# Two segments' closing work on VectorE issued behind the next segment's last key tile

## The chip, the cores and the metric

The kernel runs on one core of a Trainium2 chip. The metric is the device time of one execution in microseconds (us). Five engines each work through a queue of their own in a fixed order: TensorE (PE) multiplies matrices into PSUM, VectorE (DVE) and ScalarE (ACT) read PSUM and work on SBUF, GpSimd (POOL) fills and loads a little, and SyncE (SP) issues most DMA transfers. They wait for each other through semaphores. An instruction that waits holds up everything behind it in its own queue.

## The reference

Two attention layers over 2048 tokens, 32 heads of width 18, are computed and laid side by side. Layer A has one key and value head for all query heads; layer B splits the tokens into four segments of 512 and carries a memory from one to the next:

```python
# A: p = softmax(q k^T * Dh**-0.5) over all 2048 keys; out_A = (p v) wo
for s in range(4):                        # B, one segment of 512 tokens
    p = softmax(qs ks^T * scale + mask)
    a_dot = p vs
    pq = phi(qs)                          # phi(t) = t + 1 if t > 0 else exp(t)
    a_mem = (pq M) / (pq z + 1e-6)
    outs.append(g * a_mem + (1 - g) * a_dot)
    pk = phi(ks)
    M = M + pk^T vs                       # the memory, per head 18 x 18
    z = z + pk.sum(over tokens)
# out = concat(out_A, concat(outs) wo_B)
```

## The kernel before, in words

The program has two stages. The first (to about 289 us) computes all projections, and the second runs the attention blocks, the divisions and the output products from a table that is written out by hand. The change touches the first stage alone. The two are divided by a branch (L627, L628), which every engine passes.

In the first stage the order on each engine is not written by hand. A scheduler takes the instructions as the program issues them, with their dependencies, and lays each engine's queue out ahead of time. What the program issues earlier tends to stand earlier; an instruction that is issued in another place can therefore move many others. `tc.issue_after(x)` makes what is issued inside it depend on `x`. `pin` keeps an instruction in program order.

The loop at L414 does one segment `s` of layer B per turn:

- **Five key tiles** `t` (L449). `proj` (L253) multiplies 14 pairs of rounded parts into a PSUM tile `pj` of 126 x 512. There are four buffers of `pj`, so a tile's first matmul waits until the tile four places earlier has been read. Of `pj`, VectorE takes the maximum of each row (`kmB`, L459) and a masked copy of it (`kbB`, L463); ScalarE rounds it and VectorE forms the remainder (`qp`, L122 and L123, stored to `kB` or `qB` by SP at L127). Then `phi` (L394 to L401) runs two steps on ScalarE (`ph_e`, L397 and L398) and one on VectorE (L400, result `kf`, for the last tile `qf`). These steps take turns on one `pj`, so each waits for the one before it.
- In the next turn of `t`, `natural` (L424) transposes `kf` on TensorE into the one PSUM buffer `tr` (L427), and VectorE copies that to `pkN` (L428). Behind the five tiles `natural` does the same for `qf`, and L519 transposes `kn` into the same buffer `tr`.
- **The next segment's input**, `xr`, has three buffers of 128 x 512. SP loads it (L196), and VectorE rounds it (`xh`, L209) and forms the remainder (`xl`, L215; L217 for the short last part). A buffer can be loaded again when the remainder is formed.
- **Values** (L493): eight tiles of 14 matmuls (L503), copied to `vch` by ScalarE (L505).
- **Four query tiles** (L539): `proj` again, with `aq` (L433), `qp`, and for `s` > 0 `phi`, result `qf`.
- **The close of the segment.** TensorE forms `pu` (PSUM buffer `nd`, L566) and the memory products `pm` (PSUM buffer `mm`, L592). Of `pu`, VectorE makes the shifts: `fm` (L567), `sht` (L132) and two steps on `shp` (L134, L135), and SP stores `shB` (L571). Of `pm` it gathers the memory: L601, for `s` > 0 a sum L608, seven copies to `Mst` (L613), `zc` (L614) and five `zst` (L616), and SP stores `mzB` (L618, L619).

In segments 1 and 2 the memory is only stored for later (`from_memory`, L435, in these segments stores `qf` to `qfB`). Segment 3 reads `Mst` and `zst` directly.

Of the kernel before, what the change touches and what calls it, by code (L numbers as in the profile page):

```python
# [8 lines left out]
F32 = mybir.dt.float32  # L9
# [5 lines left out]
ALU = mybir.AluOpType  # L15
AX = mybir.AxisListType
# [5 lines left out]
NSEG, L = 4, 512  # L22
C = 512
# [38 lines left out]
LATE_ASK, ASK = (1, 2), 20  # L62


def below(rows, r0):
    return slice(rows.start + r0, rows.stop + r0, rows.step)
# [9 lines left out]
def attention_pair_kernel(ctx, tc, a_xT, a_w, a_wo, b_xT, b_w, b_wo, b_beta, ident_d, hmask_d, bmask_d, cmask_d, sel_d, zmask_d, selx_d, sely_d, out):  # L76
    nc = tc.nc
# [8 lines left out]
    qA = [dram(f"qA{c}", [H, DH, 2, C], F32) for c in range(NCH)]  # L86
    kA = dram("kA", [DH, 2, S], F32)
# [4 lines left out]
    shA = [shAs[:, H * c : H * c + H] for c in range(NCH)]  # L92
# [12 lines left out]
    ones_d = dram("ones_d", [2, S], F32)  # L105
# [23 lines left out]
    def shift_parts(pool, u, neg_scale, n, R):  # L129

        t = pool.tile([128, C], F32, name="sht", bufs=1)
        nc.vector.tensor_scalar(t[:R, :n], u, neg_scale, None, op0=ALU.mult)  # L132
        sp = pool.tile([128, 2, C], F32R, name="shp", bufs=1)
        nc.vector.tensor_copy(sp[:R, 0, :n], t[:R, :n])  # L134
        nc.vector.tensor_tensor(sp[:R, 1, :n], t[:R, :n], sp[:R, 0, :n].bitcast(F32), op=ALU.subtract)  # L135
        return sp

    def load_q(st, q, h0):

        for hf, r0 in enumerate(HALF):  # L140
            hs = slice(h0 + hf, h0 + 8, 2)
            nc.sync.dma_start(st[r0 : r0 + 36].bitcast(F32), q[hs].rearrange("h d j t -> (d j) h t"))
            nc.sync.dma_start(st[r0 + 36 : r0 + 54].bitcast(F32), q[hs, :, 0, :].rearrange("h d t -> d h t"))

# [12 lines left out]
    with ExitStack() as ph:  # L157
# [236 lines left out]
        def phi(src, R, nm, bufs, hold=lambda ins: ins):  # L394

            e = p2.tile([128, C], F32, name="ph_e", bufs=2)
            hold(nc.scalar.activation(e[:R], src, AF.Relu, scale=-1.0))  # L397
            hold(nc.scalar.activation(e[:R], e[:R], AF.Exp, scale=-1.0))  # L398
            f = p2.tile([128, C], F32, name=nm, bufs=bufs)
            hold(nc.vector.scalar_tensor_tensor(f[:R], src, 0.0, e[:R], op0=ALU.max, op1=ALU.add))  # L400
            return f  # L401

        def loose_flag():

            fm1 = pt.tile([128, 1], F32, name="fm1", bufs=1)
            nc.vector.tensor_reduce(fm1, fm, axis=AX.X, op=ALU.max)
            pf = ps.tile([128, C], F32, name="nd", bufs=2)
            nc.tensor.transpose(pf[0:1, 0:128], fm1, ident)
            fm2 = pt.tile([1, 2], F32, name="fm2", bufs=1)
            nc.vector.tensor_reduce(fm2[:, 0:1], pf[0:1, 0:128], axis=AX.X, op=ALU.max)  # L410
            nc.vector.tensor_scalar(fm2[:, 1:2], fm2[:, 0:1], float(BOUND_OK), None, op0=ALU.is_gt)
            nc.vector.tensor_copy(flag, fm2[:, 1:2])

        for s in range(NSEG):  # L414
            xh, xl = nx[:2]
            last = s == NSEG - 1
# [18 lines left out]
            def from_memory(t):  # L435
                R = RT[t]
                if s in LATE_ASK:
                    nc.sync.dma_start(qfB[s][:R, t], fs[t][:R])
                    return
                pn = ps.tile([128, C], F32, name="mm", bufs=1)  # L440
                nc.tensor.matmul(
                    pn[:R], Mst[:R, t].rearrange("p h d -> p (h d)")[:, :R], fs[t][:R], start=True, stop=True
                )
                nm = p2.tile([128, C], F32, name="nm", bufs=2)
                nc.vector.tensor_scalar(nm[:R], pn[:R], gt[:R, t : t + 1], None, op0=ALU.mult)
                nc.sync.dma_start(numB[s][126 * t : 126 * t + R], nm[:R])
# [30 lines left out]
                        load_wpart(11 + t)  # L477
            if s:
                from_memory(4)
            if s == 0:  # L480
                nc.vector.memset(gt, 0.0)
                for t, lo, hi, n in [(t, H0[t], H0[t] + HT[t], DH) for t in range(5)] + [(5, 0, 28, 4), (6, 28, 32, 32)]:
                    pin(
                        nc.gpsimd.dma_start(
                            gt[: n * (hi - lo), t : t + 1], b_beta[lo:hi][:, None].to_broadcast([hi - lo, n])[:, :, None]
                        )
                    )
# [76 lines left out]
            for t in range(5):  # L564
                R = RT[t]
                nc.tensor.matmul(pu[32 * (t % 4) : 32 * (t % 4) + 32], kbB[:R, t], aqs[t][:R], start=t < 4, stop=t > 0)  # L566
            nc.vector.tensor_reduce(fm[:, 1 + s : 2 + s], pu, axis=AX.X, op=ALU.max)  # L567
            if last:
                loose_flag()
            sp = shift_parts(pt, pu, -BOUND_UP, C, 128)  # L570
            sent = nc.sync.dma_start(shB[s].rearrange("j r t -> r j t"), sp.bitcast(F32))  # L571
            if last:
                for i in range(4):
                    values(i, 1)

            with tc.issue_after(sent.ins):
                if s == 1:
                    for r0 in HALF:
                        for rows, j in KROWS:
                            nc.sync.dma_start(kstA[below(rows, r0)].bitcast(F32), kA[:, j])  # L580
                        nc.sync.dma_start(kstA[r0 + KP : r0 + KR].bitcast(F32), ones_d)
                if s == 2:
                    load_q(st0, qA[0], 0)
                    load_shift(st0, shA[0], slice(0, 8))
            if s < NSEG - 1:
                pm = ps.tile([128, C], F32, name="mm", bufs=1)[:, : 5 * 3 * VW].rearrange("p (t m) -> p t m", t=5)
                for t in range(5):
                    for i in range(4):
                        for g in range(4 if t < 4 else 3):
                            rows = slice(32 * g, min(32 * g + 32, RT[t]))  # L590
                            h = H0[t] + FIRST[t == 4][g]
                            nc.tensor.matmul(  # L592
                                pm[rows, t],
                                pkN[:, t, i, rows],
                                vch[:, i, h : h + 3, :].rearrange("p h d -> p (h d)"),
                                start=i == 0,
                                stop=i == 3,
                            )
                new = mx if s else Mbd
                for n, (R, ts) in enumerate(((126, slice(0, 4)), (72, slice(4, 5)))):  # L600
                    nc.vector.tensor_tensor(  # L601
                        new[:R, ts].rearrange("p t h d -> p t (h d)"),
                        pm[:R, ts],
                        bands[:R, n : n + 1].rearrange("p t h d -> p t (h d)").to_broadcast([R, ts.stop - ts.start, 3 * VW]),
                        op=ALU.mult,
                    )
                if s:
                    nc.vector.tensor_tensor(Mbd[:126], Mbd[:126], mx[:126], op=ALU.add)  # L608
                for ts in (slice(0, 4), slice(4, 5)):
                    for g in range(4 if ts.start < 4 else 3):  # L610
                        rows = slice(32 * g, min(32 * g + 32, RT[ts.start]))
                        w = FIRST[ts.start == 4][g]
                        nc.vector.tensor_copy(Mst[rows, ts, w : w + 3], Mbd[rows, ts, :, 1:VW])  # L613
                nc.vector.tensor_reduce(zc[:126], Mbd[:126, :, :, 0], axis=AX.X, op=ALU.add)  # L614
                for t in range(5):
                    nc.vector.tensor_scalar(zst[: RT[t], t], zmask[: RT[t], t], zc[: RT[t], t : t + 1], None, op0=ALU.mult)  # L616
                if s + 1 in LATE_ASK:
                    nc.sync.dma_start(mzB[:, s, :, :126], Mst.rearrange("p t h d -> p t (h d)"))  # L618
                    nc.sync.dma_start(mzB[:, s, :, 126:], zst)  # L619
            if s == 0:  # L620
                pin(nc.scalar.activation(gt, gt, AF.Exp, scale=-1.0))
                pin(nc.vector.tensor_scalar(gt, gt, 1.0, None, op0=ALU.add))
# [685 lines left out]
```

## Time and profile before

| what | number |
|---|---|
| median of 3 runs | 1407.49 us (1407.48 to 1408.29) |
| the profiled execution's own time | 1409.33 us |
| its span, first to last instruction | 1407.6 us |
| granted TensorE clock, mean | 0.996 |
| TensorE busy over the span | 99% |
| VectorE busy over the span | 74% |
| ScalarE busy over the span | 85% |
| first stage ends (branch, L628) | about 289 us |

A row of the timeline gives the start, the duration, the engine, the line, the operation and how often it is merged; in brackets stands how long the engine was idle just before, and what released it. Matmuls are pipelined: they start about 0.23 us apart though each is shown with 0.39 us. A row of the windows gives each engine's busy time in a stretch, then the granted clock (PEclk), the share of DMA engines that are busy and GB/s.

### The profile page before, as it was taken

The numbers are of one execution on the slowest core, as the hardware profiler recorded it, in microseconds if no ns is written. First come the engines' busy times: TensorE is split into PE (matmuls) and PEld (weight loads), VectorE is DVE, ScalarE is ACT, GpSimd is POOL, SyncE is SP. The second block draws the span as 40 slices with busy tenths as digits, with TensorE's granted clock in tenths as the row PEclk, the third lists the DMA queues.
The fourth block names the chain that finished last, engine by engine and source line by source line (L and its number), as shares of the span: only waits on it lengthen the run. The fifth ranks groups of instructions, "written<-read, shape, count | busy, mean of one in ns | idle before, by whom it ended". The sixth has DMA issues, their size and how long they took to land.

```text
span 1407.6 us, 41232 instructions
## 1 busy us (share of the span) xinstructions
PE 1387.5 (99%) x17468; PEld 839.3 (60%) x17468; DVE 1045.2 (74%) x1557; ACT 1198.5 (85%) x1479; POOL 233.5 (17%) x335
## 2 busy tenths in 40 slices
PE   9999999989999999999999999999999999999998
PEld 6787888745554555555555555555555555555558
DVE  6656456466787779687878878777879778887883
ACT  4543434479999999999999999999999999999991
POOL 2442000003302310412110122113010220001002
PEclk9999999989999999999999999999999999999999
DMA  9766546567465345332312452333103321120022
GB/s 273 259 214 189 168 145 221 182 176 229 138 202 181 118 130 182 103 115 85 112 58 71 133 158 60 94 105 92 51 30 96 110 75 43 31 68 18 18 67 105
DMA packets 90726, 172.70 MB, mean 123 GB/s; under 512 B 14576, under 2 KB 22889, under 8 KB 90110
## 3 DMA queue, kind: packets, MB, share of 16 engines
q1 hardware_dynamic: 84122, 160.01, 36.7%
q0 software_dynamic: 1664, 4.78, 1.3%
q10 hardware_dynamic: 4752, 5.24, 1.1%
q8 instruction: 138, 2.26, 0.7%
q14 instruction: 50, 0.41, 0.1%
HBM read 99.32 MB, written 70.67 MB: 121 GB/s over the span
## 4 chain that ended last, share of the span: by engine, by line
PE 66%; DVE 4%; DMA 3%; ACT 3%; issue 2%; SPq 1%; POOL 0%; DVEq 0%; ACTq 0%
PE O L996 31%; PE E L948 19%; PE F L799 11%; ACT P L966 3%; PE E L956 3%; DVE W L963 2%; PE E L1209 2%; DMA stA<-qA 1%; DMA stB<-shB 1%; DMA stB<-qB 1%; PE F L855 1%; DMA oB<-oe 1%; DVE sm L748 0%; DVE PD L928 0%; DMA stB<-kB 0%
## 5 line engine op out<-in xcount | busy, mean ns | idle before, releaser
L966 ACT ACTIVATE P<-E 128x1024 f32<-128x1024 f32 (+1 forms) x800 | 786.7, 1073 | 4.7 <-PE E L948 4.5
L963 DVE COPY W<-E 128x1024 f32<-128x1024 f32 (+2 forms) x416 | 453.3, 1090 | 144.5 <-PE E L948 84.7
L996 PE MATMUL O<-P,VA 128*32 128x256 f32 x7504 | 508.1, 380 | 0.0
L966 ACT ACTIVATE P<-W 128x1024 f32<-128x1024 f32 (+1 forms) x330 | 369.2, 1119 | 5.8 <-DVE W L963 5.4
L996 PEld LDWEIGHTS O<-P,VA 128*32 128x32 f32 x7504 | 259.2, 110 | 138.7 <-issue 6.1
L948 PE MATMUL E<-stA,kstA 56*128 56x512 f32 x1920 | 316.9, 430 | 2.0 <-ACT P L966 1.8
L948 PEld LDWEIGHTS E<-stA,kstA 56*128 56x128 f32 x1920 | 155.0, 184 | 158.6 <-issue 94.6
L971 POOL TENSOR_SCALAR_AFFINE_SELECT P<-P 128x256 f32<-128x256 f32 (+1 forms) x192 | 94.6, 493 | 415.0 <-ACT P L966 376.8
L783 POOL TENSOR_TENSOR o<-o,rb 126x512 f32<-126x512 f32 (+1 forms) x55 | 72.9, 1351 | 438.1 <-DVE PD L929 185.1
L799 PE MATMUL F<-woB,o 126*32 126x192 f32 (+1 forms) x1920 | 126.6, 338 | 0.0
L996 PE MATMUL O<-PD,VA 128*32 128x256 f32 x688 | 88.9, 379 | 0.0
L799 PEld LDWEIGHTS F<-woB,o 126*32 126x32 f32 (+1 forms) x1920 | 38.6, 108 | 74.9 <-issue 69.7
L996 PE MATMUL O<-P,vseg 128*32 128x256 f32 (+2 forms) x1536 | 81.4, 344 | 0.1
L922 DVE TENSOR_SCALAR PD<-E 128x512 uint32<-128x512 f32 x86 | 59.2, 689 | 24.7 <-PE E L948 16.1
L1005 DVE COPY oe<-O 128x512 f32<-128x512 f32 x64 | 44.3, 692 | 42.5 <-PE O L996 41.5
L253 PE MATMUL pj<-xh,wBh 128*126 128x512 f32 x180 | 72.1, 401 | 0.0
L253 PE MATMUL pj<-xh,wBl 128*126 128x512 f32 x180 | 71.5, 397 | 0.0
L122 ACT CAST qp<-pj 126x512 fp32r<-126x512 f32 (+1 forms) x54 | 31.0, 583 | 43.1 <-DVE kmB L459 26.8
L123 DVE TENSOR_TENSOR qp<-pj,qp 126x512 fp32r<-126x512 f32 (+1 forms) x54 | 36.8, 685 | 37.5 <-ACT qp L122 37.5
L799 PE MATMUL F<-woA,o 126*32 126x192 f32 (+1 forms) x960 | 63.9, 338 | 0.0
L996 PEld LDWEIGHTS O<-P,vseg 128*32 128x32 f32 x1536 | 48.8, 109 | 24.5 <-issue 1.9
L956 PE MATMUL E<-stB 56*128 56x256 f32 (+3 forms) x512 | 61.4, 348 | 2.0 <-ACT P L966 1.3
(198 smaller groups left out, 1575.1 us busy)
## 6 DMA issues: line engine op xcount, KB each, us to landing
stB<-kB SPq DMA_DIRECT2D x96, 144.0 KB
stB<-qB SPq DMA_DIRECT2D x32, 288.0 KB
stA<-qA SPq DMA_DIRECT2D x30, 288.0 KB
oA<-oe SPq DMA_DIRECT2D x32, 256.0 KB
oB<-oe SPq DMA_DIRECT2D x32, 256.0 KB
qA<-qp SPq DMA_DIRECT2D x16, 504.0 KB
kB<-qp SPq DMA_DIRECT2D x16, 504.0 KB
qB<-qp SPq DMA_DIRECT2D x16, 504.0 KB
```

The lines of the kernel that those rows point to most:

```text
L123: hold(nc.vector.tensor_tensor(qp[:R, 1, :n], src, qp[:R, 0, :n].bitcast(F32), op=ALU.subtract))
L253: nc.tensor.matmul(dst, w[:, c0 : c0 + M], x, start=i == 0, stop=i == len(ops) - 1)
L783: ins = tc.keep_in_program_order(nc.gpsimd.tensor_tensor(dst, a, b, op=op))
L799: nc.tensor.matmul(dst[32 * j : 32 * j + 32], parts[ab, c][: RT[t], t, r0 : r0 + 32], wo[ab][: RT[t], t, c0 : c0 + n], start=start, stop=stop,
L922: v.tensor_scalar(y, e, EXP_A, EXP_B, op0=ALU.mult, op1=ALU.add)
L948: nc.tensor.matmul(e[:, j], kstA[rows, 128 * kt : 128 * kt + 128], st[rows, h, :], start=True, stop=True)
L956: nc.tensor.matmul(e[:, j, c0 : c0 + 512 - 128 * k], st[rows, 4 + h, ks], st[rows, h, 128 * k :], start=True, stop=True)
L963: gate.append(nc.vector.tensor_copy(src[:, hs, :n], e[:, hs, :n]))
L966: nc.scalar.activation(p[:, hs, :n], src[:, hs, :n], AF.Exp, scale=SCALE)
L971: nc.gpsimd.affine_select(diag, diag, pattern=[[0, 2], [0, m], [1, 128]], base=0, channel_multiplier=-1, compare_op=ALU.is_ge, fill=0.0)
L996: nc.tensor.matmul(o[32 * j : 32 * j + 32, q0 : q0 + n], v, p[:, j % 2, p0 : p0 + n], start=m == hf == 0, stop=last and hf == 1,)
L1005: nc.vector.tensor_copy(osb, o)
```

## The change

The close of a segment is put into two functions, `shifts` (from L567 to the loads behind the store of `shB`) and `collect` (L599 to L619). In segments 0 and 1 they are kept in a list and issued in the next turn of the loop, behind its five key tiles, as dependent on the last tile's `phi` (`summed`). The last one in is taken first, so `collect` comes ahead of `shifts`. In segment 2 both are issued where they were; segment 3 has only the shifts, where they were. No instruction is added or removed; `pu` and `pm` stay in their place on TensorE.

```diff
-            hold(nc.vector.scalar_tensor_tensor(f[:R], src, 0.0, e[:R], op0=ALU.max, op1=ALU.add))
+            summed[:] = [hold(nc.vector.scalar_tensor_tensor(f[:R], src, 0.0, e[:R], op0=ALU.max, op1=ALU.add))]
...
+        rest, summed = [], []
         for s in range(NSEG):
...
             if s:
                 from_memory(4)
+                with tc.issue_after(summed[0].ins):
+                    while rest:
+                        rest.pop()()
...
+            def shifts(s=s, pu=pu, last=last):
+                nc.vector.tensor_reduce(fm[:, 1 + s : 2 + s], pu, axis=AX.X, op=ALU.max)
+                if last:
+                    loose_flag()
+                sp = shift_parts(pt, pu, -BOUND_UP, C, 128)
+                sent = nc.sync.dma_start(shB[s].rearrange("j r t -> r j t"), sp.bitcast(F32))
+                with tc.issue_after(sent.ins):
+                    if s == 1:
...
+                    if s == 2:
...
             if last:
+                shifts()
                 for i in range(4):
                     values(i, 1)
+            elif s == NSEG - 2:
+                shifts()
+            else:
+                rest.append(shifts)
...
+                def collect(s=s, pm=pm):
...
+                if s == NSEG - 2:
+                    collect()
+                else:
+                    rest.append(collect)
```

Three places of the queues matter. In all rows the digits behind a name number its buffer: `pj_1418` before and `pj_1394` after are the same tile, the first key tile of segment 1.

**First place: VectorE where segment 1 begins.** Before, the shifts stand among the loads (`xh_856`, `xl_857`) of segment 1's input, and the memory copies follow:

```order
L567 TENSOR_REDUCE fm_124<-nd_1302 128x1 [waits PE_49]
L123 TENSOR_TENSOR qp_1289<-pj_1272,qp_1289 126x512 [waits DMAHW0_49,Activation_49]
L209 CAST xh_856<-xr_1293 128x512 [waits DMAHW1_49]
L132 TENSOR_SCALAR sht_1309<-nd_1302 128x512
L215 TENSOR_TENSOR xl_857<-xr_1293,xh_856 128x512 [waits DVE_49]
L209 CAST xh_856<-xr_1297 128x512 [waits DMAHW4_49,DMAHW3_49]
L134 CAST shp_1311<-sht_1309 128x512 [waits DMAHW5_49,DVE_49]
L217 TENSOR_TENSOR xh_856<-xr_1297,xh_856 64x512 [waits DVE_49]
```

After, the same stretch holds the loads of segment 2's input (`xh_1389`, `xl_1390`) ahead of the first maximum `kmB`:

```order
L215 TENSOR_TENSOR xl_1390<-xr_1415,xh_1389 128x512 [waits DVE_49]
L639 RECIPROCAL gt_121<-gt_121 128x7 [waits DVE_49]
L640 TENSOR_SCALAR omg_122<-gt_121 128x7 [waits DVE_49]
L209 CAST xh_1389<-xr_1451 128x512 [waits DMAHW0_49]
L215 TENSOR_TENSOR xl_1390<-xr_1451,xh_1389 128x512 [waits DVE_49]
L460 TENSOR_REDUCE kmB_1391<-pj_1394 126x1 [waits PE_49]
L209 CAST xh_1389<-xr_1487 128x512 [waits DMAHW1_49]
L464 TENSOR_SCALAR kbB_1392<-zmask_155,kmB_1391 126x32 [waits DVE_49]
```

The shifts and the memory copies are gone from here, and a cast that waits for a DMA of segment 2's input (`xr_1451`) now stands ahead of `kmB`.

**Second place: VectorE where the key tiles of segment 1 end.** After, the moved work stands between `qf` and the copy of its transposes out of `tr`:

```order
L625 TENSOR_REDUCE zc_855<-Mbd_839 126x5
L572 TENSOR_REDUCE fm_124<-nd_1302 128x1
L627 TENSOR_SCALAR zst_842<-zmask_155,zc_855 126x32 [waits DVE_49,Pool_49]
L627 TENSOR_SCALAR zst_842<-zmask_155,zc_855 126x32 x3
L627 TENSOR_SCALAR zst_842<-zmask_155,zc_855 72x32
L132 TENSOR_SCALAR sht_1590<-nd_1302 128x512
L429 COPY pkN_1393<-tr_1617 128x4x54 [waits PE_49]
L134 CAST shp_1592<-sht_1590 128x512 [waits DVE_49]
```

Before, that copy (L428 of `tr_1617`) came directly behind `qf`.

**Third place: VectorE where segment 2 ends and segment 3 begins.** Here `qp_2410`, `qf_2417` belong to query tile 2 of segment 2 (`pj_2393`), `qp_2437`, `qf_2444` to query tile 3 (`pj_2420`), and `pj_2562`, `pj_2583`, `pj_2604` are the first three key tiles of segment 3. Before:

```order
L567 TENSOR_REDUCE fm_124<-nd_2447 128x1 [waits PE_49]
L123 TENSOR_TENSOR qp_2410<-pj_2393,qp_2410 126x512 [waits DMAHW0_49,Activation_49]
L132 TENSOR_SCALAR sht_2454<-nd_2447 128x512
L123 TENSOR_TENSOR qp_2437<-pj_2420,qp_2437 126x512 [waits DMAHW1_49,Activation_49]
L134 CAST shp_2456<-sht_2454 128x512 [waits DVE_49]
L400 SCALAR_TENSOR_TENSOR qf_2417<-pj_2393,ph_e_2414 126x512 [waits Activation_49]
L135 TENSOR_TENSOR shp_2456<-sht_2454,shp_2456 128x512 [waits DVE_49]
L400 SCALAR_TENSOR_TENSOR qf_2444<-pj_2420,ph_e_2441 126x512 [waits Activation_49]
```

After:

```order
L460 TENSOR_REDUCE kmB_2559<-pj_2562 126x1 [waits PE_49]
L464 TENSOR_SCALAR kbB_2560<-zmask_155,kmB_2559 126x32 [waits DVE_49]
L460 TENSOR_REDUCE kmB_2559<-pj_2583 126x1 [waits PE_49]
L464 TENSOR_SCALAR kbB_2560<-zmask_155,kmB_2559 126x32 [waits DVE_49]
L123 TENSOR_TENSOR qp_2410<-pj_2393,qp_2410 126x512 [waits DMAHW0_49,Activation_49]
L123 TENSOR_TENSOR qp_2437<-pj_2420,qp_2437 126x512 [waits DMAHW1_49,Activation_49]
L400 SCALAR_TENSOR_TENSOR qf_2417<-pj_2393,ph_e_2414 126x512 [waits Activation_49]
L400 SCALAR_TENSOR_TENSOR qf_2444<-pj_2420,ph_e_2441 126x512 [waits Activation_49]
```

The work on query tiles 2 and 3 now stands behind all shifts and memory copies of segment 2 (those rows are directly ahead of the ones shown) and behind the maxima of the first two key tiles of segment 3. The scheduler made this move; the diff does not ask for it.

More of the change, by code (lines that the diff above doesn't have):

```diff
@@ L566, in attention_pair_kernel @@
                 nc.tensor.matmul(pu[32 * (t % 4) : 32 * (t % 4) + 32], kbB[:R, t], aqs[t][:R], start=t < 4, stop=t > 0)
-            nc.vector.tensor_reduce(fm[:, 1 + s : 2 + s], pu, axis=AX.X, op=ALU.max)
+            def shifts(s=s, pu=pu, last=last):
[6 more added lines that the diff above has]
+                    if s == 1:
+                        for r0 in HALF:
+                            for rows, j in KROWS:
+                                nc.sync.dma_start(kstA[below(rows, r0)].bitcast(F32), kA[:, j])
+                            nc.sync.dma_start(kstA[r0 + KP : r0 + KR].bitcast(F32), ones_d)
+                    if s == 2:
+                        load_q(st0, qA[0], 0)
+                        load_shift(st0, shA[0], slice(0, 8))
             if last:
[L569 to L572, printed above, removed]
+                shifts()
                 for i in range(4):
                     values(i, 1)
[L576 to L584, printed above, removed]
+            elif s == NSEG - 2:
+                shifts()
+            else:
+                rest.append(shifts)
             if s < NSEG - 1:
@@ L598, in attention_pair_kernel @@
                             )
[L599 to L619, printed above, removed]
+                def collect(s=s, pm=pm):
+                    new = mx if s else Mbd
+                    for n, (R, ts) in enumerate(((126, slice(0, 4)), (72, slice(4, 5)))):
+                        nc.vector.tensor_tensor(
+                            new[:R, ts].rearrange("p t h d -> p t (h d)"),
+                            pm[:R, ts],
+                            bands[:R, n : n + 1].rearrange("p t h d -> p t (h d)").to_broadcast([R, ts.stop - ts.start, 3 * VW]),
+                            op=ALU.mult,
+                        )
+                    if s:
+                        nc.vector.tensor_tensor(Mbd[:126], Mbd[:126], mx[:126], op=ALU.add)
+                    for ts in (slice(0, 4), slice(4, 5)):
+                        for g in range(4 if ts.start < 4 else 3):
+                            rows = slice(32 * g, min(32 * g + 32, RT[ts.start]))
+                            w = FIRST[ts.start == 4][g]
+                            nc.vector.tensor_copy(Mst[rows, ts, w : w + 3], Mbd[rows, ts, :, 1:VW])
+                    nc.vector.tensor_reduce(zc[:126], Mbd[:126, :, :, 0], axis=AX.X, op=ALU.add)
+                    for t in range(5):
+                        nc.vector.tensor_scalar(zst[: RT[t], t], zmask[: RT[t], t], zc[: RT[t], t : t + 1], None, op0=ALU.mult)
+                    if s + 1 in LATE_ASK:
+                        nc.sync.dma_start(mzB[:, s, :, :126], Mst.rearrange("p t h d -> p t (h d)"))
+                        nc.sync.dma_start(mzB[:, s, :, 126:], zst)
```

## Prediction

> **What bounds the kernel now.** I read the page's busy times first, then busy time by stretch around the places where segments meet, then TensorE's waits, and then the timelines of the engines there. The first row is from the page, the others are stretches of the first stage: microseconds, then each engine's busy time, the granted clock, the DMA share and GB/s.
>
> ```profile
> PE 1387.5 (99%) x17468; PEld 839.3 (60%) x17468; DVE 1045.2 (74%) x1557; ACT 1198.5 (85%) x1479; POOL 233.5 (17%) x335
> ```
>
> ```profile
> 127.00:136.00 9.00, 9.00 (x167) 7.57 (x158) 8.29 (x25) 0.78 (x3) 0.35 (x1) 1.00 0.71 231
> 136.00:160.00 24.00, 22.20 (x137) 19.47 (x137) 18.59 (x42) 11.75 (x27) 0.00 (x0) 1.00 0.74 209
> 184.00:194.00 10.00, 9.03 (x42) 7.05 (x41) 9.87 (x29) 3.57 (x7) 0.00 (x0) 1.00 0.51 167
> ```
>
> TensorE is at work for 99% of the span. VectorE is nearly full only where segments meet (8.29 of 9 us, 9.87 of 10), and there TensorE is idle twice: 24 − 22.20 = 1.80 us and 10 − 9.03 = 0.97 us. The table of waits and TensorE's timeline name the cause; in a row of waits stand the sum, the count and the longest.
>
> ```profile
> PE tr L427 <- DVE kf L400: 2.8, 2, 1.8
> ```
>
> ```profile
> 139.17 0.62 PE L427 MATMUL tr<-ident,kf 126*128 126x126 f32 x4 [1.80 <-DVE kf L400]
> ...
> 191.84 0.65 PE L427 MATMUL tr<-ident,kf 126*128 126x126 f32 x4 [0.97 <-DVE kf L400]
> ```
>
> Both are the transposes of a segment's first `kf`, late because VectorE had the closing work to do first. So the change can win at most 1.80 + 0.97 = 2.8 us. Whatever it adds to TensorE's waits in stage 1 delays everything behind, since stage 2 begins with the branch. No instruction is added or removed; the sum is one of waits. All clock times below are those of the profiled run before.
>
> **Term 1, the wait at 139 us.** VectorE's rows there:
>
> ```profile
> 127.21 0.69 DVE L567 TENSOR_REDUCE fm<-nd 128x1 f32<-128x512 f32 x1 [1.48 <-PE nd L566]
> ...
> 128.75 0.68 DVE L132 TENSOR_SCALAR sht<-nd 128x512 f32<-128x512 f32 x1
> 129.35 0.68 DVE L215 TENSOR_TENSOR xl<-xr,xh 128x512 fp32r<-128x512 f32 x1
> ...
> 134.77 0.68 DVE L459 TENSOR_REDUCE kmB<-pj 126x1 f32<-126x512 f32 x1
> ...
> 138.34 0.69 DVE L400 SCALAR_TENSOR_TENSOR kf<-pj,ph_e 126x512 f32<-126x512 f32 x1
> ```
>
> With the memory and shifts gone, `kmB` would start some 4 us earlier and the wait would vanish, but the order puts a cast of `xr_1451` ahead of `kmB`, and that waits for a load into a buffer that the remainder (L215) frees. SyncE issues such a load as soon as L215 ends (129.35 + 0.68 = 130.03):
>
> ```profile
> 130.06 1.76 SPq L196 DMA_DIRECT2D xr<-b_xT  x2
> ```
>
> After the change L215 is ready earlier by what stood ahead: `fm` (about 0.5 of its slot) and `sht` (0.60, to L215's start), so about 1.05, and the load goes out at 129.0. How long it takes to land the trace does not show for this load. The nearest rows are loads of 252 KB (this one has 256 KB) from GpSimd's queue, the median of four and the fastest, in the summary of DMA issues of two stretches:
>
> ```profile
> wr<-b_w POOLq DMA_DIRECT2D x4, 252.0 KB, 4.0
> ```
>
> ```profile
> wr<-b_w POOLq DMA_DIRECT2D x1, 252.0 KB, 2.9
> ```
>
> and, for a late one, a load of the same kind in a busier stretch, from issue to the cast that waited for it:
>
> ```profile
> 55.64 0.54 SPq L196 DMA_DIRECT2D xr<-b_xT  x1
> ```
>
> ```profile
> 61.26 0.89 DVE L209 CAST xh<-xr 128x512 fp32r<-128x512 f32 x1 [0.98 <-DMA xr<-b_xT]
> ```
>
> That is 5.6 us. I take 4.0, nearest in size and the median, and keep 2.9 and 5.6. Then the load is there at 133.0, the cast and the remainder take 0.4 + 0.7, and `kmB` starts at 134.1, 0.67 us earlier than before. From `kmB` to `kf` the same steps alternate with ScalarE (138.34 − 134.77 = 3.57 us before); with another cast between them up to 0.3 is lost again. **−0.5 us.** By 2.9 it is −1.6, by 5.6 it is +1.1.
>
> **Term 2, the wait at 191 us.** The same mechanism one segment on:
>
> ```profile
> 180.66 0.68 DVE L567 TENSOR_REDUCE fm<-nd 128x1 f32<-128x512 f32 x1
> ...
> 187.48 0.68 DVE L459 TENSOR_REDUCE kmB<-pj 126x1 f32<-126x512 f32 x1
> ```
>
> The remainder takes the slot of `fm` and ends at 181.34; its buffer's load lands 4.0 later at 185.4, and with cast and remainder `kmB` starts at 186.4, 1.1 earlier. But the order of TensorE has these transposes behind 7 projections instead of 11, four matmuls or 0.93 us earlier (0.23 apart, rows in term 4). **−0.1 us**; by 2.9 −0.97 (all of it), by 5.6 +1.5.
>
> **Term 3, the moved work.** It now stands between `qf` and the copy of its transposes (`pkN`). There is one `tr`, so the transposes of `kn` (L519) wait for that copy. Rows of the parts, of VectorE and then TensorE:
>
> ```profile
> 132.06 0.51 DVE L601 TENSOR_TENSOR Mbd<-mm,bands 126x228 f32<-126x228 f32 x2
> 132.90 1.74 DVE L613 COPY Mst<-Mbd 32x216 f32<-32x216 f32 x7 [0.34 <-DVE Mbd L601]
> ...
> 135.37 0.81 DVE L616 TENSOR_SCALAR zst<-zmask,zc 126x32 f32<-126x32 f32 x5
> ...
> 153.15 0.69 DVE L400 SCALAR_TENSOR_TENSOR qf<-pj,ph_e 126x512 f32<-126x512 f32 x1 [0.41 <-ACT ph_e L398]
> 154.65 0.38 DVE L428 COPY pkN<-tr 128x216 f32<-128x216 f32 x1 [0.81 <-PE tr L427]
> ```
>
> ```profile
> 148.40 0.30 PE L503 MATMUL pj<-wBh,xh 128*128 128x306 f32 x1
> ...
> 149.92 0.30 PE L503 MATMUL pj<-wBl,xh 128*128 128x306 f32 x1
> ...
> 153.99 0.62 PE L427 MATMUL tr<-ident,qf 126*128 126x126 f32 x4
> ```
>
> In segment 1 stand there L601 with its gap and the copies (132.06 to about 134.67, 2.61), `zc` (0.10 in its slot), `fm` (0.60), `zst` (0.72), `sht` (0.60) and the copy itself (0.38): 5.0 us, from 153.75 to 158.8, with a signal of 0.1 158.9. TensorE gets there after its transposes (0.36) and 25 value matmuls of (149.92 − 148.40)/11 = 0.138, at 153.99 + 0.36 + 3.5 + 0.1 for a small one between = 158.0. **+0.9 us** (0 if `qf` comes that much earlier, as it waits for ScalarE; 1.3 at most, if TensorE meets no gap). In segment 2 there are a sum and both steps on `shp` more, 5.7 to 6.2 us, against 0.36 + 35 × 0.138 = 5.2: **+0.6 us** (0 to 1.1).
>
> **Term 4, segment 3's third key tile.** `pj` has four buffers, so `pj_2604` takes that of `pj_2393`, query tile 2 of segment 2, and its first matmul waits for `qf_2417`. Before, that was done at 235.5, long before the tile began. After, it stands behind `kmB` of `pj_2583`, which needs the last matmul of the tile directly ahead of `pj_2604`. TensorE must then wait out a chain through VectorE and ScalarE, however early they are:
>
> ```profile
> 239.73 0.39 PE L253 MATMUL pj<-xh,wBl 128*126 128x512 f32 x1
> 239.96 0.40 PE L253 MATMUL pj<-xh,wBh 128*126 128x512 f32 x1
> ...
> 246.22 0.39 PE L253 MATMUL pj<-xh,wBl 128*126 128x512 f32 x1
> ```
>
> ```profile
> 234.82 0.68 DVE L400 SCALAR_TENSOR_TENSOR qf<-pj,ph_e 126x512 f32<-126x512 f32 x1
> ...
> 242.03 0.24 DVE L463 TENSOR_SCALAR kbB<-zmask,kmB 126x32 bf16<-126x32 f32 x1
> ...
> 246.65 0.69 DVE L459 TENSOR_REDUCE kmB<-pj 126x1 f32<-126x512 f32 x1 [1.23 <-PE pj L253]
> ```
>
> ```profile
> 233.41 0.60 ACT L397 ACTIVATE ph_e<-pj 126x512 f32<-126x512 f32 x1 [0.76 <-DVE qp L123]
> ...
> 242.03 0.58 ACT L122 CAST qp<-pj 126x512 fp32r<-126x512 f32 x1 [3.69 <-DVE kmB L459]
> ```
>
> A free VectorE starts `kmB` 246.65 − 246.22 = 0.43 after a tile's last matmul, so at 240.16. Then `kmB` and `kbB` (0.69 + about 0.2, to 241.05), `qp_2410` (0.69 like the others, to 241.74), ScalarE's first step (0.5 until the next can start) and its cast for `qp_2437` (0.58, to 242.86), `qp_2437` (0.60 until the next starts), and `qf_2417` (0.68, to 244.18), 0.1 for the signal: 244.28. TensorE would have begun at 239.96: **+4.3 us**. What is queued behind on TensorE is the rest of stage 1, and nothing there can run ahead. The closing work of segment 2, all of it ahead of `kmB` now, is done at about 239, so it adds nothing.
>
> **Term 5, the clock.** TensorE waited for the branch at the end of stage 1, and behind it the granted clock was halved:
>
> ```profile
> 289.12 1.35 PE L948 MATMUL E<-st,kstA 56*128 56x512 f32 x4 [1.58 <-SPq L628]
> ```
>
> ```profile
> 290.00:293.00 3.00, 2.09 (x9) 0.81 (x5) 1.96 (x4) 1.81 (x2) 0.14 (x1) 0.50 0.06 16
> ...
> 296.00:299.00 3.00, 3.00 (x26) 0.99 (x24) 2.51 (x3) 3.00 (x4) 0.00 (x0) 0.50 0.78 176
> 299.00:302.00 3.00, 3.00 (x36) 1.72 (x34) 1.78 (x4) 2.38 (x4) 0.00 (x0) 0.85 0.60 172
> ```
>
> The clock stayed at 1.00 over the 1.80 us at 139, but fell at 290 after 1.58 and further short gaps, and came back at 299.9 ((1 − 0.85)/0.5 × 3 = 0.9 us into the last stretch), 3.5 us after TensorE was full again. A wait of 4.3 us is longer than either, so I expect the fall here, and 3.5 us at half clock lose half: **+1.7 us** (0 without it; 3.5 if it lasts twice as long).
>
> [...]
>
> **The sum.** −0.5 − 0.1 + 0.9 + 0.6 + 4.3 + 1.7 = **+6.9 us**. The profiled execution took 1409.33 us, so its like would be 1416.2; the median is 1.84 lower, 1407.49, and the forecast goes by that: **1414.4 us**.
>
> **The rivals.**
> 1. The clock holds over the 4.3 us, as it did over 1.80 us: +5.2, 1412.7. For it speaks 139 us, against it 290 us.
> 2. Late loads, 5.6 us as at 55: terms 1 and 2 become +1.1 and +1.5, the sum +10.1, 1417.6. For it speaks the DMA share of 0.71 to 0.74 there, against it the median of 4.0.
> 3. **Not slower:** fast loads. From 2.9 us down the load no longer sets `kmB`; both old waits go (−2.8), `qf` comes early enough to keep term 3 at nothing, and with the clock held only term 4 is left: +1.5, 1409.0. It decides at a landing of about 2.9 us. If the clock also stayed up past the branch, where it ran at half for 10.2 us before (up to 5.1 us), the time would be 1403.9.
> 4. That the change does nothing is excluded by the order of the queues: the wait of `pj_2604` is in it.
>
> **How the numbers follow.** Forecast 0.46; clock holds 0.27; late loads 0.13; fast loads 0.10, and with the clock past the branch 0.04. A measurement can tell about 0.2% of this kernel from no change, 2.8 us: 1404.7 to 1410.3 counts as the same. Faster is only the last case, 0.04; same are the fast loads and some of the clock rival between 2.9 and 4.0 us, 0.13; slower 0.83. The range goes from the fast loads, 1409.0, to the late ones, 1417.6.
>
> **What would show it.** Before `tr` from the first `kf` the idle time should be 1.3 in segment 1 and 0.9 in segment 2; L523 should wait for `pkN` about 0.9 and 0.6; before a matmul on `pj` in segment 3 a new idle time of 4.3 us should be put down to `qf`, with a clock of 0.5 behind it; stage 1 should end at about 296 instead of 289. The prediction is wrong if `kmB` of segment 1 comes near 131 (no load ahead of it), if the wait of `pj_2604` is below 3 us, or if stage 2 takes another time than before.

## The result and the profile after

The changed kernel takes **1420.0 us** (median of 6 runs, 1419.72 to 1420.78) against 1408.2 for the kernel before (6 runs beside it): a ratio of 1.0082, 95% interval 1.0071 to 1.0093. It is slower by 11.8 us; 6.9 were forecast, and 1420.0 lies above the forecast range, which ended at 1417.6.

TensorE's waits in the changed kernel (in total, times, longest; the edits shift the line numbers a little from kernel to kernel):

```profile
PE pj L253 <- DVE qf L400: 4.1, 1, 4.1
...
PE tr L428 <- DVE kbB L464: 2.5, 1, 2.5
PE tr L428 <- DVE kf L400: 2.0, 1, 2.0
PE E L964 <- issue: 2.0, 1, 2.0
```

The new wait on `qf` is there at the size forecast. The two waits before the first `kf` transposes, 1.80 and 0.97 us before, are longer, not shorter (the one that names `kbB` ended with the instruction directly behind `kf`). No wait of the transposes of `kn` (L523) is in the table. The three places on TensorE's timeline, and the `kn` transposes of segment 3:

```profile
138.27 0.62 PE L428 MATMUL tr<-ident,kf 126*128 126x126 f32 x4 [2.54 <-DVE kbB L464]
...
192.68 0.65 PE L428 MATMUL tr<-ident,kf 126*128 126x126 f32 x4 [1.96 <-DVE kf L400]
...
247.70 0.50 PE L253 MATMUL pj<-xh,wBh 128*126 128x512 f32 x1 [4.08 <-DVE qf L400]
...
267.02 0.49 PE L523 MATMUL tr<-ident,kn 128*18 128x128 f32 x3
```

The granted clock (third number from the right) fell behind each of the three waits, not only behind the last:

```profile
139.00:140.00 1.00, 1.00 (x4) 0.80 (x3) 0.97 (x3) 0.97 (x2) 0.00 (x0) 0.52 0.76 254
142.00:143.00 1.00, 1.00 (x5) 0.79 (x4) 0.00 (x0) 0.59 (x1) 0.00 (x0) 0.78 0.61 197
193.00:194.00 1.00, 1.00 (x7) 0.85 (x5) 1.00 (x2) 0.60 (x1) 0.00 (x0) 0.82 0.00 0
248.00:249.00 1.00, 1.00 (x4) 0.81 (x3) 0.63 (x2) 1.00 (x3) 0.00 (x0) 0.63 0.48 150
```

Inside the three stretches the clock reads 0.50 (139.10 to 142.40, 193.70 to 197.00, 248.30 to 251.60) and around them 1.00, so a share s of a microsecond in a stretch gives a mean of 1 − s/2. So the clock fell at 139.04, 193.64 and 248.26, and the first fall ended at 142.44. That is 3.40 us at half clock, and by an estimate, half of it, 1.7 us lost where TensorE has work throughout. Behind the third wait it shows: from the tile's first matmul to the `kn` transposes it took 267.02 − 247.70 = 19.32 us, before 257.63 − 239.96 = 17.67, so 1.65 more. The other two falls ended at 197.06 and 251.68, as long after their begin.

**Where the 11.8 us are.** Each seam is measured between two marks, so that all it contains is in it. Marks are the starts of the same matmuls on both timelines:

| mark | before | after | difference | added since the mark above |
|---|---|---|---|---|
| first projection of segment 1 | 128.81 | 127.14 | −1.67 | |
| `pu` of segment 1 | 178.82 | 179.58 | +0.76 | +2.43 |
| `pu` of segment 2 | 230.84 | 234.10 | +3.26 | +2.50 |
| `kn` transposes of segment 3 | 257.63 | 267.02 | +9.39 | +6.13 |
| first matmul of stage 2 | 289.12 | 298.42 | +9.30 | −0.09 |
| second group of stage 2 | 291.39 | 301.32 | +9.93 | +0.63 |
| end of the span | 1407.6 | 1418.0 | +10.4 | +0.5 |

The −1.67 belongs to the profiled executions, not to the kernels. Nothing that the change touches stands there; most of it comes from the first matmuls of the kernel, which ran slowly in the execution of before (before, then after):

```profile
6.25 2.02 PE L285 MATMUL pj<-xh,wAh 128*114 128x512 f32 x4 [0.68 <-DVE wAh L226]
```

```profile
6.18 1.16 PE L285 MATMUL pj<-xh,wAh 128*114 128x512 f32 x4 [0.61 <-DVE wAh L226]
```

The two rows account for 0.93 us; by the start of the fourth group of this kind (11.39 before, 9.93 after) the difference is 1.46. Why they ran slowly is not known. Without the 1.67 the two differ by 12.1 us, near the 11.8 of the medians. The longer waits are 0.74 + 0.99 + 4.08 = 5.8 us, three stretches at half clock 3 × 1.7 = 5.1, the begin of stage 2 and the rest 0.6 + 0.5. These terms come to 12.0. Of the last two the cause is not settled: the wait put down to "issue" at the begin of stage 2, 0.91 us before and 1.96 after, was 1.3 to 1.8 in those experiments whose table of waits lists it, the one that is faster than before included.

**Why the heads' waits grew.** VectorE and SyncE where segment 1 begins, in the changed kernel:

```profile
127.35 8.27 SPq L196 DMA_DIRECT2D xr<-b_xT  x6
```

```profile
132.43 0.43 DVE L209 CAST xh<-xr 128x512 fp32r<-128x512 f32 x1 [1.60 <-DMA xr<-b_xT]
132.89 0.69 DVE L215 TENSOR_TENSOR xl<-xr,xh 128x512 fp32r<-128x512 f32 x1
133.50 0.69 DVE L460 TENSOR_REDUCE kmB<-pj 126x1 f32<-126x512 f32 x1
...
137.44 0.68 DVE L400 SCALAR_TENSOR_TENSOR kf<-pj,ph_e 126x512 f32<-126x512 f32 x1
```

The first of the six loads (`xr_1451`) was issued at 127.35, which is 129.02 on the clock of the prediction (+1.67; it said 129.0), and the cast began 5.08 us later, not 4.0. So `kmB` began at 135.17 by that clock instead of 134.1, behind the 134.77 of before. From `kmB` to `kf` it took 3.94 us against 3.57. VectorE itself stood idle for 1.60 us ahead of that cast, with `kmB` ready behind it. In segment 2 the same: a load issued at 182.13 and cast at 187.02, 4.89 us.

```profile
182.13 0.37 SPq L196 DMA_DIRECT2D xr<-b_xT  x1
```

```profile
187.02 0.43 DVE L209 CAST xh<-xr 128x512 fp32r<-128x512 f32 x1 [2.78 <-DMA xr<-b_xT]
```

### The profile page after: what moved, and what is told of

Read it like the earlier page. It is cut to its first block, busy times and chain, and to the rows that moved or that the text cites. A ratio compares the mean times of both kernels' runs of the same rounds, so it can differ in the third digit from the quotient of the medians.

```text
span 1418.0 us, 41230 instructions
## 1 busy us (share of the span) xinstructions
PE 1391.1 (98%) x17468; PEld 841.6 (59%) x17468; DVE 1045.9 (74%) x1557; ACT 1199.5 (85%) x1479; POOL 233.6 (16%) x335
## 4 chain that ended last, share of the span: by engine, by line
PE 68%; ACT 5%; DVE 4%; issue 2%; POOL 0%; ACTq 0%; DVEq 0%
PE O L1012 31%; PE E L964 19%; PE F L815 11%; ACT P L982 4%; PE E L972 3%; DVE W L979 2%; PE E L1225 2%; PE F L871 1%; DVE sm L764 0%; DVE PD L944 0%; DVE PD L942 0%; PE F L1225 0%; PE O L1225 0%; DVE o L876 0%; DVE PD L943 0%
```

## The experiments

**The theory** to test: the heads' waits hang on the load ahead of `kmB` alone, the third on the place of `qf_2417`, and the rest of the loss is the half clock that such waits bring. The rivals: the waits come with the moved work whatever the order, and the clock falls for another reason.

| kernel | time, us | before beside it | ratio, 95% interval |
|---|---|---|---|
| casts behind `kmB` | 1411.92 | 1407.91 | 1.0030 (1.0017 to 1.0042) |
| query tiles first | 1412.28 | 1407.91 | 1.0024 (1.0014 to 1.0035) |
| both edits | 1405.46 | 1407.91 | 0.9984 (0.9975 to 0.9993) |
| filler, 10 matmuls | 1417.86 | 1407.91 | 1.0072 (1.0059 to 1.0086) |
| segment 0 deferred only | 1410.56 | 1407.50 | 1.0019 (1.0009 to 1.0029) |
| segment 1 deferred only | 1415.35 | 1407.50 | 1.0052 (1.0035 to 1.0069) |
| shifts deferred only | 1413.81 | 1407.50 | 1.0044 (1.0028 to 1.0061) |
| filler, 13 matmuls | 1418.49 | 1407.50 | 1.0068 (1.0050 to 1.0087) |

### The load out of the way

```diff
-            rounded = (nc.scalar.copy if ... else nc.vector.tensor_copy)(xh[:, k], xr)
+            with tc.issue_after(after) if after is not None else nullcontext():
+                rounded = (nc.scalar.copy if ... else nc.vector.tensor_copy)(xh[:, k], xr)
...
-                hold(nc.vector.tensor_reduce(kmB[...], pj[:126], ...))
+                big = hold(nc.vector.tensor_reduce(kmB[...], pj[:126], ...))
...
-                    nx[2](t)
+                    nx[2](t, after=big.ins)
```

> The changed kernel, with one edit: each cast of the next segment's input is ordered behind the maximum kmB of its own key tile, so that no load stands ahead of the first kmB of segments 1 and 2. Theory: the two waits before the first kf transposes (2.54 and 1.96 us in the changed kernel) hang on that load alone. They go, and with them the two stretches of 3.4 us at half clock behind them (1.7 each); the wait of 4.1 us in segment 3 and its half clock stay. 1420.0 - 4.5 - 3.4 = 1412.1 us. Rival A, the waits come from somewhere else (the moved work, ScalarE): both stay, 1420. Rival B, the half clock does not come from these waits: only the waits go, 1415.5.

1411.92 us, as the theory has it (1412.1). The one long wait in its first stage, and the stretches in which the changed kernel lost its clock at the two heads:

```profile
PE pj L254 <- DVE qf L401: 4.1, 1, 4.1
```

```profile
130.00:140.00 10.00, 10.00 (x49) 7.99 (x48) 8.36 (x17) 4.23 (x7) 0.00 (x0) 1.00 0.53 180
140.00:150.00 10.00, 10.00 (x62) 8.98 (x61) 8.41 (x16) 5.76 (x12) 0.00 (x0) 1.00 0.66 201
...
190.00:200.00 10.00, 10.00 (x60) 8.81 (x59) 9.63 (x19) 5.07 (x10) 0.00 (x0) 1.00 0.45 134
```

No wait for the first `kf` is left, TensorE is busy through these stretches and the clock is 1.00. The deferral itself therefore does what it can do, 2.8 us; the casts that the scheduler put into the gap took it back. Rival A falls, and B with it: the clock stayed up where the wait went. The edit moved more than the one cast: the other casts and remainders of the next segment's input stand later too, among them two pairs that stood between `kmB` and `kf`. So this run alone does not show that the first load decides; the next run adds to that.

### The third wait

```diff
             elif s == NSEG - 2:
-                shifts()
+                with tc.issue_after(summed[0].ins):
+                    shifts()
...
                 if s == NSEG - 2:
-                    collect()
+                    with tc.issue_after(summed[0].ins):
+                        collect()
...
+                with tc.issue_after(summed[0].ins) if last and t < 2 else nullcontext():
                     hold(nc.vector.tensor_reduce(kmB[...], pj[:126], ...))
```

> The changed kernel, with one edit: VectorE's closing work of segment 2 and the first two maxima of segment 3 are ordered behind qf of the last query tile of segment 2. Theory: the wait of 4.1 us before segment 3's third key tile hangs on qf_2417 standing behind kmB of the tile ahead. It goes, with the half clock behind it (about 2.0 us); the two waits at the segments' heads stay. 1420.0 - 4.1 - 2.0 = 1413.9 us. Rival A: the closing work, now behind, delays segment 3's maxima, and a wait of 2 us or more comes at a later key tile: 1416 to 1418. Rival B, the half clock would come anyway: 1415.9.

1412.28 us (8 runs, 1408.74 to 1414.82), 1.6 below the expectation. No wait on `qf` is left and none has come in its place. The runs spread over 6.1 us, and the mean granted clock goes with them: 0.997 in the fastest, 0.993 in the slowest, and 0.004 of 1411 us is 5.6 us (an estimate from rounded clocks). Only the slowest has a trace, and there it is the first head that is late:

```profile
PE tr L428 <- DVE kbB L465: 3.7, 1, 3.7
...
PE tr L428 <- DVE kf L400: 1.9, 1, 1.9
```

```profile
127.25 9.47 SPq L196 DMA_DIRECT2D xr<-b_xT  x6
```

```profile
133.52 0.43 DVE L209 CAST xh<-xr 128x512 fp32r<-128x512 f32 x1 [3.34 <-DMA xr<-b_xT]
```

At this place the order is that of the changed kernel. The same load was cast 6.27 us after its issue instead of 5.08, and the wait was 3.74 instead of 2.54: 1.2 later, 1.2 longer. That shows at two values that the wait hangs on this load. The half clock also lasted longer here:

```profile
137.00:138.00 1.00, 0.00 (x0) 0.00 (x0) 0.97 (x3) 0.97 (x2) 0.00 (x0) 0.84 0.96 170
144.00:145.00 1.00, 1.00 (x5) 0.70 (x4) 0.00 (x0) 0.34 (x1) 0.00 (x0) 0.75 0.46 168
195.00:196.00 1.00, 1.00 (x6) 0.86 (x5) 0.88 (x2) 0.73 (x2) 0.00 (x0) 0.85 0.00 0
```

It began at 137.68, while TensorE still waited (to 139.36), and ended at 144.50, so 5.1 us of work ran at half clock behind this wait instead of 3.4.

### Both edits together

> Both edits of the two runs before it. Theory: all three waits and the half clock behind each are gone, and the old waits of 1.80 and 0.97 us too: 1420.0 - 8.6 - 5.4 = 1406.0 us, and by the kernel before 1408.2 - 2.8 = 1405.4 us, so faster than both kernels by 0.2%. Rival: with the loads' casts behind kmB the next segment's input comes late, and TensorE waits where segment 2 begins: 1408 or more.

1405.46 us, the 1405.4 that the sum by the kernel before gives: of the three waits 0.2 us on one `kf` is all that the table has left, and the kernel is faster than before by 0.16% (0.07 to 0.25). It is the fastest of all kernels here. The rival, input that comes late, isn't there.

### Work in place of idle time

```diff
+                    if last and t == 2:
+                        busy = ps.tile([128, 4, 128], F32, name="tr", bufs=1)
+                        with tc.issue_after(made[-1].ins):
+                            for _ in range(10):
+                                spin = nc.tensor.matmul(busy..., wBh[:, 0, 0:126], xh[:, 0], ...)
+                    with tc.issue_after(spin.ins) if last and t == 2 else nullcontext():
                         proj(...)
```

> The changed kernel, with ten matmuls of 126x512 added on TensorE directly ahead of segment 3's third key tile; their result is not used. They take 10 x 0.23 = 2.3 us of the wait of 4.1 us there, and nothing else stands otherwise. Theory: the clock falls for want of work, so with 1.8 us of it left it stays at full speed behind this wait, and the kernel gets faster by added work: 1420.0 - 1.9 = 1418.1 us, and the pj row behind the filler shows an idle time of about 1.8. Rival A, the half clock has another cause than the idle time: 1420.0. Rival B, 1.8 us of idle time is enough to halve the clock (it was not before, at 139 us): 1420.0 with the clock at 0.5 behind it.

1417.86 us is the number of the theory (1418.1), but not for its reason, so the agreement is luck. TensorE's rows, then the stretches:

```profile
138.32 0.62 PE L432 MATMUL tr<-ident,kf 126*128 126x126 f32 x4 [2.35 <-DVE kbB L474]
```

```profile
246.19 0.50 PE L255 MATMUL pj<-xh,wBh 128*126 128x512 f32 x1 [1.75 <-DVE qf L404]
```

```profile
130.00:140.00 10.00, 7.65 (x36) 5.96 (x35) 7.84 (x18) 3.42 (x6) 0.00 (x0) 1.00 0.59 178
140.00:150.00 10.00, 10.00 (x56) 8.27 (x55) 8.35 (x15) 4.44 (x8) 0.00 (x0) 1.00 0.60 210
...
240.00:250.00 10.00, 8.25 (x31) 6.20 (x30) 5.52 (x10) 3.79 (x7) 0.00 (x0) 0.85 0.42 140
```

Behind the 1.75 us left of the third wait the clock fell (rival B), and behind 2.35 us at the first head it did not. So this run does not say what the filler is worth, and in it the length of a wait alone did not decide on the clock (the last section has the waits of all runs). The longer filler was made to get clear of that:

> The filler ahead of segment 3's third key tile again, now with 13 matmuls (3.0 us); the result is not used. The order is that of the changed kernel up to the last query tiles of segment 3, where a few instructions change places. Theory: only about 1.1 us of the wait is left, too little to halve the clock in any period: no half clock behind it, and from the tile's first matmul to the first transposes of kn in segment 3 it takes 17.7 us as in the kernel before (239.96 to 257.63), where the changed kernel took 19.3 (247.70 to 267.02). The time is 1418 us, give or take 1.5 for the changed places and for the clock at the two heads. Rival: the half clock has another cause than the idle time: 19.3 us again.

```profile
248.39 0.50 PE L255 MATMUL pj<-xh,wBh 128*126 128x512 f32 x1 [1.05 <-DVE qf L404]
...
266.17 0.49 PE L533 MATMUL tr<-ident,kn 128*18 128x128 f32 x3
```

With 1.05 us left the clock held, and from the tile to the `kn` transposes it took 266.17 − 248.39 = 17.78 us as expected (17.7), where the changed kernel took 267.02 − 247.70 = 19.32. TensorE had three microseconds more work in the same place and lost 1.5 us less behind it. The total, 1418.49, is in the band given, which is too wide to say more: in the profiled run the first head waited 3.05 us.

### One part alone

Segment 0 alone (`elif s:` and `if s:` in place of the tests for `NSEG - 2`):

> Only segment 0's closing work is deferred (to segment 1); segments 1 and 2 close where they did before. Theory: the wait before segment 1's first kf transposes is that of the changed kernel (2 to 3.7 us, by how late xr_1451 lands, instead of 1.80) with half a period of half clock behind it (1.7 us) where it falls into one period; the other two are as before (0.97 us in segment 2, none in segment 3, where the order of VectorE is the old one). 1407.9 + 0.7 to 1.9 + 1.7 = 1410.3 to 1411.5 us. Rival: the wait in segment 3 belongs to the scheduler's whole order and comes here too: 1416 or more.

Segment 1 alone (`s != 1` there):

> Only segment 1's closing work is deferred (to segment 2); segments 0 and 2 close where they did before. Theory: the wait of 1.80 us in segment 1 is as before; in segment 2 there is that of the changed kernel (1.96 for 0.97 us, and 1.7 at half clock), and the 4.1 us in segment 3 with their 2.0 at half clock come with it: 1407.9 + 1.0 + 1.7 + 6.1 = 1416.7 us. Rival: the wait in segment 3 needs both deferrals: 1410.6.

The shifts alone (`if True:` ahead of `collect()`):

> Only the shifts are deferred (segments 0 and 1); the memory copies stay where they were before. Theory: the memory copies hold kmB back as before and the load behind it still comes, so the heads' waits are about as long as before or a little longer (about 2.1 and 1.3 us), and segment 3's third tile waits less than in the changed kernel (about 2.4 us), since the maxima there stand behind fewer instructions; the clock may fall behind the first and the third: 1407.9 + 0.6 + 2.4 + 1.7 to 3.4 = 1412.6 to 1414.3 us. Rival, the shifts alone are what stood in the way: the heads' waits go and it is 1405 to 1408.

TensorE's waits in the three, in that order:

```profile
PE tr L428 <- DVE kbB L464: 2.4, 1, 2.4
...
PE tr L428 <- DVE kf L400: 1.0, 1, 1.0
```

```profile
PE pj L253 <- DVE qf L400: 4.1, 1, 4.1
PE tr L428 <- DVE kf L400: 3.9, 2, 2.1
```

```profile
PE tr L428 <- DVE kbB L464: 2.0, 1, 2.0
PE pj L253 <- DVE qf L400: 2.0, 1, 2.0
...
PE tr L428 <- DVE kf L400: 1.1, 1, 1.1
```

With segment 0 alone only the first head's wait has grown (1410.56, expected 1410.3 to 1411.5). Segment 1 alone brings the second head's and, with it, the third wait: the scheduler reorders the end of segment 2 when segment 1's close moves, and not when segment 0's does. Its 1415.35 is 1.35 below the expectation. The missing part is the clock: the second head waited 2.10 us there and the clock stayed at 1.00, so the 1.7 counted for it was not lost. Nothing of it lies behind the branch: from the first matmul of stage 2 to the end of the span it took 1118.5 us there, as before. With the shifts alone all three waits are there in about the sizes expected (1413.81, expected 1412.6 to 1414.3): the memory copies hold `kmB` back as before. The load still stands ahead of it, but in the profiled run its cast waited only 0.16 us.

## Why the prediction was wrong

The direction and most of the mechanisms held. Two terms of the sum were mis-sized, the landing of the loads (terms 1 and 2) and the number of falls of the clock (term 5), and the first decides on the second.

- **Term 4, segment 3's third tile:** forecast 4.3, measured 4.08. The chain through VectorE and ScalarE was followed rightly, down to the rows that it was built of, and taking `qf` out of it took the wait out (query tiles first).
- **Terms 1 and 2, the heads:** forecast −0.5 and −0.1, measured +0.74 and +0.99 in the waits. The step that failed is "I take 4.0, nearest in size and the median" for the landing of a load. It took 5.08 and 4.89 us here and 6.27 in another run. The loads of 4.0 came from GpSimd's queue. The row of 5.6 was from SyncE's queue, but it was no full load of the same kind: it is the second half of a short part. The summary of issues from 55 to 57 us gives its size, and the load behind it, a full one, was issued at 57.57 (the first of the two in its row) and cast at 65.55:

```profile
xr<-b_xT SPq DMA_DIRECT2D x1, 128.0 KB
```

```profile
57.57 2.30 SPq L196 DMA_DIRECT2D xr<-b_xT  x2
```

```profile
65.55 0.43 DVE L209 CAST xh<-xr 128x512 fp32r<-128x512 f32 x1 [1.94 <-DMA xr<-b_xT]
```

That is 8.0 us, with a DMA share of 0.93 from 57 to 66. So full loads of 252 or 256 KB took from 2.9 to 8.0 us in the trace of before, and the median of four of them hid that range. That the load stands ahead of `kmB`, and that the gain hangs on it, was right: with the casts behind `kmB` both waits went.

- **Term 5, the clock:** 1.7 was forecast for one fall; there were three, 5.1 us. This is the larger miss, and it follows from the other: terms 1 and 2 gave waits of 1.3 and 0.9 us. In the first stage from 128 us on, no wait of up to 1.12 us was followed by half clock in any trace here (0.97, 1.05 and 1.12 were not), none lay between 1.12 and 1.75, and 2.54 and 1.96 were followed by it. The prediction asked of the wait of 4.3 us alone whether it is longer than the 1.80 us over which the clock had stood, added the clock's price to that wait alone and gave none of its ends for the heads a price for it; the rival of late loads, too, left it out. With 1.7 for each head it would have stood at 1421.0. The price itself, 1.7 for one fall, came out right by luck. The 3.5 us behind it were counted from the stretch that begins at 296, but TensorE was busy without a gap from 294.73:

```profile
294.73 1.71 PE L948 MATMUL E<-st,kstA 56*128 56x512 f32 x6 [0.64 <-ACT P L966]
```

To 299.9 that is 5.2 us, and the whole fall at 290 lasted 10.2. Nor did "further short gaps" belong to its cause. The row below puts the fall at 289.66, behind the 1.58 us alone and ahead of the next gap (290.47 to 291.39):

```profile
289.00:290.00 1.00, 0.88 (x4) 0.56 (x5) 0.00 (x0) 0.00 (x0) 0.00 (x0) 0.83 0.39 131
```

- **Term 3, the moved work behind `qf`:** forecast 0.9 and 0.6, measured about 0.1 and none. VectorE's copy ended at 159.08 in segment 1 and the transposes began at 159.14, with TensorE free about 0.1 before that. The order put the work as described, but VectorE needed 4.65 us from the end of `qf` to that of the copy, where 5.0 had been taken, and TensorE began the transposes of `qf` 1.13 us after `qf` began, where it had been 0.84 before. So the slack was just enough.
- **Stage 2** was taken to last as long as before. From its first matmul to the end of the span it took 1119.55 us instead of 1118.46, the 0.6 + 0.5 above, whose cause stays open.

## What to carry to other kernels

When work is moved out of a gap, look at what the scheduler puts there: a cast that waits for a transfer was worse here in front of a critical instruction than the work it replaced, since the engine stood idle ahead of it (1.60 and 2.78 us). A transfer's landing is a range and not a value (2.9 to 8.0 us in the trace of before), so see what lies just beyond the value taken: here one microsecond more of landing lengthened two waits and brought a fall of the clock behind each, at 1.7 us apiece. An order that ties a load's cast behind the instruction it must not hold up, and the query work ahead of the closing work, turned a loss of 11.8 us into a gain of 2.5.

## What the runs showed of the hardware

In the ten traces, in windows of 0.1 us from 128 to 330 us (the kernel before from 188, and 1.00 over 10 to 289 there), a stretch at half clock lasted 3.41, 6.83 or 10.24 us, so one, two or three times 3.41: 3.41 behind each of the three waits of the changed kernel, 6.83 from 137.68 on with the query tiles first, 10.24 from 289.66 on in the kernel before. Within an execution the falls lay a whole number of times 3.41 us apart: 54.60 and 54.62 us in the changed kernel (16 times), 58.0 with the query tiles first (137.68 and 195.70, 17 times), 51.2 with the casts behind `kmB` (241.71 and 292.91, 15 times).

TensorE's waits of more than 0.9 us in the first stage, from 128 us on to the branch, by what the clock did behind them:

| kernel | fell, us | stayed at 1.00, us |
|---|---|---|
| before | | 1.80, 0.97 |
| changed | 2.54, 1.96, 4.08 | |
| casts behind `kmB` | 4.08 | |
| query tiles first | 3.74, 1.91 | |
| both edits | | |
| filler, 10 matmuls | 1.88, 1.75 | 2.35 |
| segment 0 deferred only | 2.40 | 0.97 |
| segment 1 deferred only | 4.08 | 1.80, 2.10 |
| shifts deferred only | 2.04 | 1.12, 1.98 |
| filler, 13 matmuls | 3.05, 2.09 | 1.05 |

So behind waits of 1.75 to 2.40 us the clock fell in some cases and held in others. What sorts most of them is an estimate from the distances above: count back and forth from a fall in steps of 3.41 us, and take the idle time within one step, here called a period. With the falls as boundaries, periods end at 139.04, 193.64 and so on in the changed kernel: its waits of 2.54 us (135.73 to 138.27) and 1.96 us (190.72 to 192.68) lie in one period each, and both were followed by half clock. In the run with 10 filler matmuls and in the one with segment 1 alone the falls are in these rows:

```profile
192.00:193.00 1.00, 1.00 (x4) 0.72 (x4) 0.48 (x1) 0.97 (x2) 0.00 (x0) 0.72 0.37 123
```

```profile
244.00:245.00 1.00, 1.00 (x3) 0.81 (x4) 0.35 (x1) 1.00 (x3) 0.00 (x0) 0.50 0.25 80
```

The first fell at 192.44, so by the estimate a boundary lies 16 periods ahead at 137.8: its 2.35 us (135.97 to 138.32) are split into 1.85 and 0.5, and the clock held. The second fell at 244.0, so one would lie at 189.4: its 2.10 us (188.34 to 190.44) are split into halves, and the clock held.

```profile
190.44 0.65 PE L428 MATMUL tr<-ident,kf 126*128 126x126 f32 x4 [2.10 <-DVE kf L400]
```

The same working on all ten traces, in the first stage from 128 us on, gives this: in these runs each period with 1.88 us or more of idle time was followed by half clock (1.88 at 191 in the run with 10 filler matmuls is the least), and none with 1.23 or less (1.23 of the 4.08 in the changed kernel, ahead of 244.85, is the most). Between the two it is not settled: 1.80 us in one period (before, at 139, and with segment 1 alone) and 1.85 were not followed by it, but the 1.75 us behind the filler were. At the branch the clock fell behind 1.58 us in the kernel before and behind 1.45 in the one with both edits, but not behind 1.46 with the query tiles first, so the idle time of a period does not sort these. The ends of matmuls are modelled, so tenths are not to be read closely. Behind a wait of about 2 us the loss in these runs was thus none (1.98, 2.10 and 2.35) or that of 3.41 us at half clock (1.96, 2.04, 2.09 and 2.40), which is 1.7 by the estimate above. A longer wait cost more in one run: behind the 3.74 us with the query tiles first, 5.1 us of work at half clock are 2.6 lost by the same estimate. In that kernel the spread of the runs goes with the granted clock, and a landing after 6.27 us instead of 5.08 went with a wait of 3.74 instead of 2.54. How much of the spread of each kernel comes from the landing and how much from where a wait lies against the falls was not tried.
